# Second batch's scores in float32 from raw q and k in a fused attention, dense and routed layer kernel

## The chip, the cores and the metric

The kernel runs on one core of one Trainium2 chip. The metric is the time of one execution on the device in microseconds, as the median of several runs. Engines are named as in the profile: PE is TensorE (PEld its weight loads), DVE is VectorE, ACT is ScalarE, POOL is GpSimd, and SP is SyncE, which issues most transfers.

## The reference, cut to what matters

```
# q, k, v: float32 (4 batches, 8 heads, 576 positions, 64 wide)
scores = matmul(q, k.T) / 8
kth    = the 32nd largest score of each row
attn   = softmax over the scores >= kth (the others are masked)
x      = attn @ v, heads laid side by side: 2304 rows of 512

x = ((x @ w_a) * (x @ w_b)) @ w_out                 # 512 -> 1536 -> 512
e = argmax(x @ w_gate); g = its softmax weight       # 8 experts
out = g * (relu(x @ w1[e]) @ w2[e])                  # 512 -> 1024 -> 512
```

Which scores pass as the 32 largest, and which expert a row goes to, depend on small differences. So the kernel keeps products near float32 accuracy: it either feeds TensorE float32 operands, or splits an operand into a rounded part and a remainder and adds three cheaper products.

## The kernel before

The work runs in three layers: attention of the four batches, the dense layer of the four batches (`moe1`), and the eight experts (`expert`).

**Attention.** It is cut into units of one pair of heads: batch 0 has eight (its two groups of rows are units of their own, 320 and 256 rows), batches 1 to 3 have four each. A unit's q and k come by DMA as `rawq` and `rawk` (128 partitions, one head on each half, two buffers each). TensorE makes the scores of one half of the columns for both heads at a time, into the only buffer `sp` in PSUM (`score`, L521; L502 for the last 64 rows of both heads, the M tile). This is called a score step below; a pair of heads has eight of the first kind, and one for its M tile. ScalarE copies `sp` to `s` (L527), VectorE forms pairwise maxima and minima `m` and `n` (L535), finds the 32nd largest by MAX8 and MATCH_REPLACE8 (L546 to L573), and masks (L601, which reads the scores `s` and the exponentials `e`, both in SBUF). TensorE transposes the masked rows (L627) and multiplies by v (L648); the result is normalized and written to `xf`.

**How q and k are fed.** `prep_unit` has two ways, chosen by `u.f`, that is by the unit's number in `FU`. With `u.f`, the scores are one float32 product from `rawq` and `rawk`. Without it, ScalarE rounds each to `kH` and `qH` (L464), GpSimd forms the remainders `kL` and `qL` (L465), and a score step has three products, kH·qH, kH·qL and kL·qH. `FU` is `range(8)`: batch 0 alone has the first way. A float32 product stands in the trace as two records, each of the other three as one.

**The dense layer as fill.** When a batch's attention is done, its dense layer gives TensorE 576 matmuls on L748 and 288 on L778, in runs of six; these are called fills below. They are placed between the next batch's attention work. The fills of batch 0 also need the float64 weights, which are converted on the chip during batches 0 and 1 (`conv`, ACT L383/L387, VectorE L385/L388, GpSimd L391/L397) and stored to `ws` and `wos` in DRAM. The fills of batch 3 and the experts follow the attention.

**What sets the order.** No order is written out. Every step is recorded with an engine, a cost and a place `pos`; `Plan.emit` then steps through its own model of the engines, each time giving a free engine the ready step with the lowest `pos`, and the resulting order is what each engine executes. Attention steps have `pos` from 0 up, fills 1e5 more, so that attention goes first where both are ready. `score` is given a cost of 780 with `u.f` and 540 without; the split steps have costs of their own. Changing them shifts the whole order behind. Each engine executes its order strictly, so a step that waits holds up all behind it on its engine.

```
    P(PE, 780 if u.f else 540, pos, score, r=u.q + u.k, w=[sp], label=f"score{u.b}")
```

Of the kernel before, what the change touches and what calls it, by code (L numbers as in the profile page):

```python
# [209 lines left out]
def fused_kernel(ctx: ExitStack, tc: tile.TileContext, q, k, v, w_a, w_b, w_out, w_gate, w1, w2, qx, kx, vx, out,  # L210
                 opts=None, dbg=None):
    nc = tc.nc
    opts = opts or {}
# [15 lines left out]
    HB = FB // 2  # L229
    CW = 512  # L230
    HALVES = opts.get("halves", (0,))
    FU = opts.get("fu", range(8))
    PE, ACT, DVE, POOL, SP = "PE", "ACT", "DVE", "POOL", "SP"

    dram = ctx.enter_context(tc.tile_pool(name="dram", bufs=1, space=bass.MemoryType.DRAM))
# [192 lines left out]
    def load_unit(ui, b, p, groups, pos, after=None):  # L428

        u = Rec()  # L430
        u.b, u.p, u.f, u.first = b, p, ui in FU, ui == 0
        u.raw = {}
# [1105 lines left out]
```

## Time and profile before

| | |
|---|---|
| median of 3 runs | 1207.14 us (1203.96 to 1209.49) |
| profiled execution, its own time | 1207.8 us |
| its span | 1206.1 us |
| PE busy | 1082.9 us, 90% of the span, 7586 instructions |
| DVE busy | 894.5 us, 74% |
| ACT busy | 678.6 us, 56% |
| POOL busy | 462.5 us, 38% |
| chain that ended last | PE 53%, DVE 23%, issue 9%, DMA 6%, ACT 4%, POOL 3% |

Busy shares are means over stages with different limits, so they are read by stretch. In the trace, the scores of batch 0 run until 204 us, those of batch 1 from 211 to 398, and the attention of the other two ends near 788. Up to about 300 us VectorE is busy all the time and TensorE is not; from 344 on TensorE is nearly always busy.

### The profile page before, as it was taken

The page shows a single profiled execution, that of the slowest core. Times are in us where ns is not written, and L with a number is a line of the kernel's source. Part 1 is how long each engine was busy: PE and PEld are TensorE (multiplying, and loading weights), DVE is VectorE, ACT ScalarE, POOL GpSimd, SP SyncE. Part 2 cuts the span into 40 slices and gives each one's busy share as a digit, 9 for nine tenths or more (in the row PEclk, how much of TensorE's full clock was granted, in tenths as well). Part 3 has the DMA queues.
Part 4 walks back from the last instruction along what each step waited for, and adds up shares of the span by engine and source line. Part 5 has one row for each costly group of instructions (what it writes and reads, how often), then busy time and mean ns, then how long its engine had stood idle before and what let it go on. Part 6 is the DMA issues. An engine that isn't in the chain of part 4 may idle for free.

```text
span 1206.1 us, 21828 instructions
## 1 busy us (share of the span) xinstructions
PE 1082.9 (90%) x7586; PEld 942.3 (78%) x7586; DVE 894.5 (74%) x2636; ACT 678.6 (56%) x1442; POOL 462.5 (38%) x620
## 2 busy tenths in 40 slices
PE   3555696887999999999999999998999999999997
PEld 1333474765788789889888888898998999999996
DVE  6999999999989999999999999920005554544441
ACT  6667676775666666666666655723224454554551
POOL 3555577654445444134646313535134100000001
PEclk9766796987999999999999999999999999999999
DMA  7586577996666423333334242245735555554450
GB/s 260 172 311 200 177 250 252 364 311 205 233 235 208 171 96 114 135 115 120 130 104 137 79 144 78 80 167 206 253 126 177 180 151 191 179 163 148 160 177 21
DMA packets 90476, 210.47 MB, mean 175 GB/s; under 512 B 7363, under 2 KB 44611, under 8 KB 82677
## 3 DMA queue, kind: packets, MB, share of 16 engines
q1 hardware_dynamic: 87141, 199.53, 49.2%
q0 software_dynamic: 3216, 9.46, 2.1%
q8 instruction: 62, 1.02, 0.3%
q14 instruction: 57, 0.47, 0.1%
HBM read 174.31 MB, written 35.25 MB: 174 GB/s over the span
## 4 chain that ended last, share of the span: by engine, by line
PE 53%; DVE 23%; issue 9%; DMA 6%; ACT 4%; POOL 3%; SPq 0%; POOLq 0%; DVEq 0%; ACTq 0%
PE ab L748 18%; PE ab L778 10%; DVE m L559 5%; PE ab L1109 4%; DVE kt L562 4%; DVE am L601 4%; PE pv L648 3%; PE sp L521 3%; PE tp L627 3%; PE ms L1158 2%; PE pv L1158 2%; DMA xsort<-rows,pi 2%; DMA out_dram<-y,ti 2%; DVE m L535 1%; DVE n L535 1%
## 5 line engine op out<-in xcount | busy, mean ns | idle before, releaser
L748 PE MATMUL ab<-xh,wt 128*128 128x320 f32 (+1 forms) x1344 | 302.9, 306 | 3.9 <-ACT sb L733 3.9
L748 PEld LDWEIGHTS ab<-xh,wt 128*128 128x128 f32 x1344 | 226.3, 191 | 17.8 <-issue 11.1
L748 PE MATMUL ab<-xl,wt 128*128 128x320 f32 (+1 forms) x672 | 200.0, 298 | 1.4 <-POOL xl L718 1.4
L559 DVE MATCH_REPLACE8 m<-kt,m 128x288 f32<-128x288 f32 x432 | 188.5, 440 | 0.0
L562 DVE MAX8 kt<-m 128x8 f32<-128x288 f32 x432 | 182.1, 444 | 0.4
L778 PE MATMUL ab<-gH,wt 128*128 128x320 f32 (+1 forms) x768 | 169.4, 304 | 2.9 <-DMA wt<-wos 2.9
L756 POOL TENSOR_TENSOR sa<-sa,sb 128x320 f32<-128x320 f32 (+1 forms) x96 | 82.9, 864 | 154.9 <-ACT sb L733 147.8
L601 DVE SCALAR_TENSOR_TENSOR am<-s,kt,e 128x576 f32<-128x576 f32 x144 | 137.9, 983 | 0.0
L778 PEld LDWEIGHTS ab<-gH,wt 128*128 128x128 f32 x768 | 127.8, 190 | 10.7 <-issue 6.4
L748 PEld LDWEIGHTS ab<-xl,wt 128*128 128x128 f32 x672 | 128.9, 192 | 1.6 <-POOL xl L718 1.6
L554 ACT ACTIVATE e<-s,nm 128x576 f32<-128x576 f32 x144 | 108.9, 781 | 16.8 <-POOL nm L549 15.6
L778 PE MATMUL ab<-gT,wt 128*128 128x320 f32 (+1 forms) x384 | 113.8, 296 | 0.0
L1183 POOL DMA_INDIRECT out_dram<-y,ti x23 | 22.9, 997 | 227.6 <-ACT y L1177 208.7
L1027 DVE TENSOR_TENSOR wp<-raw,wp 128x1024 fp32r<-128x1024 f32 (+1 forms) x73 | 67.4, 943 | 52.8 <-ACT wp L1026 52.6
L527 ACT COPY s<-sp 128x576 f32<-128x576 f32 x128 | 81.9, 640 | 40.5 <-PE sp L521 37.5
L627 PE MATMUL tp<-idr,am 128*128 128x128 f32 x512 | 82.3, 299 | 19.4 <-DVE am L601 16.0
L397 POOL TENSOR_TENSOR gT<-sa,gH 128x320 fp32r<-128x320 f32 (+1 forms) x96 | 83.9, 874 | 40.6 <-ACT gH L396 40.4
L631 ACT COPY aT<-tp 128x512 f32<-128x512 f32 x128 | 71.4, 588 | 41.9 <-PE tp L627 41.6
L627 PEld LDWEIGHTS tp<-idr,am 128*128 128x128 f32 x512 | 63.0, 153 | 37.5 <-DVE am L601 18.9
L521 PE MATMUL sp<-rawk,rawq 64*128 64x288 f32 x128 | 37.6, 666 | 60.3 <-DVE n L534 21.9
L1109 PE MATMUL ab<-xgh,wp 128*128 128x304 f32 (+6 forms) x352 | 89.8, 313 | 1.5 <-DVE gT L1116 0.9
L648 PE MATMUL pv<-aT,vt 128*64 128x320 f32 (+1 forms) x512 | 80.4, 458 | 4.2 <-ACT aT L616 3.4
(280 smaller groups left out, 2409.0 us busy)
## 6 DMA issues: line engine op xcount, KB each, us to landing
wt<-ws SPq DMA_DIRECT2D x54, 1024.0 KB, 5.5
wt<-wos SPq DMA_DIRECT2D x44, 768.0 KB, 4.3
raw<-in_moe_w_dram SPq DMA_DIRECT2D x64, 512.0 KB, 3.8
xsort<-rows SPq DMA_DIRECT2D x8, 771.0 KB, 13.1
wp<-ws SPq DMA_DIRECT2D x6, 1024.0 KB
rawk<-in_kx_dram SPq DMA_DIRECT2D x19, 320.0 KB, 5.7
rawq<-in_qx_dram SPq DMA_DIRECT2D x19, 320.0 KB, 3.7
vt<-in_vx_dram SPq DMA_DIRECT2D x20, 288.0 KB, 2.8
```

The lines of the kernel that those rows point to most:

```text
L397: P(POOL, c_pool(cost), pos, lambda: nc.gpsimd.tensor_sub(lo(), src(), fr(hi())), r=rd + wh, w=wl)
L527: P(ACT, c_act(S), pos, lambda hf=hf, sp=sp: nc.scalar.copy(s()[:, :, hf * HS:(hf + 1) * HS], sp()[:, :, 0:HS]), r=[sp], w=[(s, (h, hf)) f ...
L554: P(ACT, c_act(S, True) + 90, pos, lambda h=h, e=e: nc.scalar.activation(e(), s()[:, h], AF.Exp, bias=nm()[:, h], scale=SCALE), r=[(s, (h, ...
L559: P(DVE, c_dve(HS), pos + 5.0 * h, lambda x=x, h=h, j=j: nc.vector.match_replace(out=m()[:, h], in_to_replace=kt(j, 8 * x - 8, 8 * x), in_ ...
L562: P(DVE, c_dve(HS), pos + 5.0 * h, lambda x=x, h=h, j=j: nc.vector.max(out=kt(j, 8 * x, 8 * x + 8), in_=m()[:, h]), r=[(m, h)], w=[KT(j, x)])
L601: P(DVE, c_dve(S) + 60, pos, lambda: nc.vector.scalar_tensor_tensor(am(), sc(), kth(), e(), op0=OP.is_ge, op1=OP.mult, accum_out=r.sum()[: ...
L627: res = nc.tensor.transpose(tp()[:, 512 * h + x * 128:512 * h + (x + 1) * 128], z()[:, 640 * h + x * 128:640 * h + (x + 1) * 128], idf)
L648: nc.tensor.matmul(pv()[64 * h:64 * h + 64, 0:n], u.vt()[:, 256 * h + 64 * j:256 * h + 64 * j + 64], r.aT[h]()[:, j, 0:n], start=(j == 0), ...
L748: res = nc.tensor.matmul(pa()[:, 0:n], view()[:, m, wi, ko, :], xv()[:, ko], start=(ko == 0 and x == 0), stop=(ko == KO - 1 and x == 2))
L756: P(POOL, c_pool(n), pos, lambda: nc.gpsimd.tensor_mul(sa()[:, 0:n], sa()[:, 0:n], sb()[:, 0:n]), r=[sb], w=[sa])
L778: res = nc.tensor.matmul(pa()[:, 0:n], wv()[:, wi, f, :], gv()[:, f, :], start=(f == 0 and x == 0), stop=(f == HB - 1 and x == 2))
L1109: res = nc.tensor.matmul(pa()[:, 0:cap], p1[ko]()[:, wi, f * 128:(f + 1) * 128], xv()[:, ko], start=(ko == 0 and i == 0), stop=(ko == KO - ...
```

## The change

`FU` becomes `range(12)`, so the four units of batch 1 (numbers 8 to 11) are fed the first way. Their eight roundings (L464) and eight remainders (L465) are gone; their 32 score steps on L521 and the 4 of their M tiles on L502 have one float32 product in place of three, and read `rawk` and `rawq`, whose buffers come free after the unit's last score instead of after its split. Batches 2 and 3 keep the split.

```diff
-    FU = opts.get("fu", range(8))
+    FU = opts.get("fu", range(12))
```

The planner makes a new order from there on. Three places follow.

TensorE in batch 1, first unit, between the M tile's score and the next score step (`xh`, `xl` and `wt` are the fill's operands, `am` a masked row that is transposed). Before, where the run of fills ends:

```order
L748 MATMUL ab<-xl_516,wt 128x320
L748 MATMUL ab<-xh_511,wt 128x320
L521 MATMUL sp<-kH,qH 128x288 x2
L521 MATMUL sp<-kH,qL 128x288 x2
L521 MATMUL sp<-kL,qH 128x288 x2
L627 MATMUL tp<-idr,am 128x128 x8
```

After, at the same score step:

```order
L748 MATMUL ab<-xl_516,wt 128x320
L748 MATMUL ab<-xh_511,wt 128x320
L521 MATMUL sp<-rawk,rawq 128x288 x2
L627 MATMUL tp<-idr,am 128x128 x8
L636 MATMUL pv<-idr,am 128x128
L748 MATMUL ab<-xh_511,wt 128x320
```

The three products are one; counted back to the M tile's score, 18 fills stand ahead of this step before, and 42 after.

GpSimd where batch 0 ends and the first units of batch 1 are prepared (L397 and L391 work on converted weights and on the dense layer, L698 on `xf`). Before:

```order
L397 TENSOR_TENSOR gT_1344<-sa,gH_1335 128x320
L465 TENSOR_TENSOR kL<-rawk,kH 128x640
L698 TENSOR_TENSOR xf<-xc,rs 128x256
L391 TENSOR_TENSOR x_1355<-x_1355,xl_1434 128x512
L756 TENSOR_TENSOR sa<-sa,sb 128x320
L465 TENSOR_TENSOR qL<-rawq,qH 128x640
L397 TENSOR_TENSOR gT_1344<-sa,gH_1335 128x320
L397 TENSOR_TENSOR xl_1434<-x_1355,xl_1434 128x512
```

After:

```order
L397 TENSOR_TENSOR gT_1344<-sa,gH_1335 128x320
L698 TENSOR_TENSOR xf<-xc,rs 128x256
L391 TENSOR_TENSOR x_1355<-x_1355,xl_1434 128x512
L756 TENSOR_TENSOR sa<-sa,sb 128x320
L397 TENSOR_TENSOR xl_1434<-x_1355,xl_1434 128x512
L397 TENSOR_TENSOR gT_1344<-sa,gH_1335 128x320
```

The two remainders are gone and the other steps close up.

TensorE at the change from batch 1 to batch 2, behind the last product with v of batch 1 (L652; the M tile is that of batch 2's first unit, with the split in both kernels). Before:

```order
L652 MATMUL pv<-aTt,vt 64x256 x2
L690 MATMUL pv<-idr,rr_101 128x128 x2
L502 MATMUL sp<-kH,qH 128x288 x2
L502 MATMUL sp<-kH,qL 128x288 x2
L502 MATMUL sp<-kL,qH 128x288 x2
L627 MATMUL tp<-idr,am 128x128 x4
L748 MATMUL ab<-xh_4286,wt 128x256
L748 MATMUL ab<-xl_4300,wt 128x256
L748 MATMUL ab<-xh_4286,wt 128x256 x2
L748 MATMUL ab<-xl_4300,wt 128x256
L748 MATMUL ab<-xh_4286,wt 128x256
L627 MATMUL tp<-idr,am 128x128 x4
```

After:

```order
L652 MATMUL pv<-aTt,vt 64x256 x2
L502 MATMUL sp<-kH,qH 128x288 x2
L502 MATMUL sp<-kH,qL 128x288 x2
L502 MATMUL sp<-kL,qH 128x288 x2
L690 MATMUL pv<-idr,rr_101 128x128 x2
L627 MATMUL tp<-idr,am 128x128 x8
L636 MATMUL pv<-idr,am 128x128
L748 MATMUL ab<-xh_4119,wt 128x256
L748 MATMUL ab<-xl_4134,wt 128x256
```

The broadcast for the norm (L690) stands behind the M tile's score now, and the transposes of both masked rows stand ahead of the first fill. Counted up to this M tile's score there are 888 fills in both kernels; up to the score step behind it 942 before and 924 after.

## Rows read from the trace of the kernel before

**Rows 1.** Busy time by stretch; header names columns, then granted clock and DMA.

```profile
core 0: us, PE busy (x) PEld busy (x) DVE busy (x) ACT busy (x) POOL busy (x), PEclk, DMA share, GB/s
184.00:211.00 27.00, 15.70 (x73) 9.35 (x73) 27.00 (x71) 15.00 (x30) 18.70 (x17) 0.62 0.72 246
...
240.00:270.00 30.00, 24.07 (x162) 19.71 (x163) 29.86 (x90) 22.93 (x51) 16.96 (x18) 0.89 0.94 311
270.00:300.00 30.00, 22.86 (x142) 18.07 (x142) 27.51 (x86) 15.88 (x31) 14.42 (x21) 0.77 0.63 205
300.00:344.00 44.00, 41.79 (x337) 35.50 (x335) 43.97 (x153) 27.24 (x63) 22.18 (x37) 1.00 0.62 218
344.00:404.00 60.00, 59.85 (x487) 50.68 (x485) 54.87 (x173) 40.52 (x95) 27.09 (x41) 1.00 0.70 248
404.00:426.00 22.00, 17.91 (x129) 13.50 (x121) 22.00 (x82) 13.30 (x29) 10.43 (x16) 0.92 0.24 81
426.00:785.00 359.00, 356.81 (x2732) 309.68 (x2730) 341.14 (x1097) 226.09 (x510) 151.44 (x217) 1.00 0.32 112
```

**Rows 2.** Waits of VectorE, 184 to 404 us: total, times, longest.

```profile
DVE m L535 <- ACT s L527: 6.8, 3, 3.8
```

**Rows 3.** Groups of instructions: the split, all three batches; busy, mean ns, idle before.

```profile
L465 POOL TENSOR_TENSOR qL<-rawq,qH 128x640 fp32r<-128x640 f32 x12 | 19.6, 1636 | 0.9 <-ACT qH L464 0.9
...
L465 POOL TENSOR_TENSOR kL<-rawk,kH 128x640 fp32r<-128x640 f32 x12 | 18.7, 1562 | 11.2 <-ACT kH L464 7.6 <-DMA wt<-ws 3.6
...
L464 ACT CAST kH<-rawk 128x640 fp32r<-128x640 f32 x12 | 8.7, 728 | 0.1
```

**Rows 4.** Timeline of POOL: start, length, and the instruction.

```profile
188.49 1.72 POOL L465 TENSOR_TENSOR qL<-rawq,qH 128x640 fp32r<-128x640 f32 x1
...
309.76 1.56 POOL L465 TENSOR_TENSOR qL<-rawq,qH 128x640 fp32r<-128x640 f32 x1
```

**Rows 5.** Timeline of DVE: L388 and L601 beside those, and apart from them.

```profile
189.10 1.66 DVE L388 SCALAR_TENSOR_TENSOR gT<-gT 128x512 int32<-128x512 int32 x1
...
213.54 0.67 DVE L388 SCALAR_TENSOR_TENSOR x<-xl,x 128x512 int32<-128x512 int32 x1
...
284.93 0.81 DVE L601 SCALAR_TENSOR_TENSOR am<-s,kt,e 128x576 f32<-128x576 f32 x1
...
310.26 1.67 DVE L601 SCALAR_TENSOR_TENSOR am<-s,kt,e 128x576 f32<-128x576 f32 x1
```

**Rows 6.** Timeline of PE: a float32 score step of batch 0 between fills.

```profile
161.70 0.31 PE L748 MATMUL ab<-xh,wt 128*128 128x320 f32 x1
161.94 0.76 PE L521 MATMUL sp<-rawk,rawq 64*128 64x288 f32 x4
162.62 0.41 PE L748 MATMUL ab<-xh,wt 128*128 128x320 f32 x1
```

**Rows 7.** Timeline of PE: a split score step of batch 1 between fills.

```profile
300.47 0.31 PE L778 MATMUL ab<-gT,wt 128*128 128x320 f32 x1
300.62 0.31 PE L778 MATMUL ab<-gH,wt 128*128 128x320 f32 x1
300.86 0.40 PE L521 MATMUL sp<-kH,qH 64*128 64x288 f32 x2
...
301.45 0.42 PE L778 MATMUL ab<-gH,wt 128*128 128x320 f32 x1
```

**Rows 8.** Timeline of PE: score steps at the lower clock, float32 first, then split.

```profile
202.79 1.33 PE L521 MATMUL sp<-rawk,rawq 64*128 64x288 f32 x4
204.28 0.69 PE L648 MATMUL pv<-aT,vt 128*64 128x256 f32 x2 [0.16 <-ACT aTt L638]
...
244.71 0.61 PE L521 MATMUL sp<-kH,qH 64*128 64x288 f32 x2 [5.00 <-DVE kt L573]
...
245.87 1.97 PE L627 MATMUL tp<-idr,am 128*128 128x128 f32 x8
```

**Rows 9.** Waits of the DMA queue SP, 205 to 420 us: total, times, longest.

```profile
SPq L435 <- POOL kL L465: 8.5, 4, 2.8
```

## The prediction

> **What bounds the kernel now.** I read the busy times by stretch first, because the shares of the whole span mix stages [rows 1]. Between 184 and 211 us VectorE is busy all 27.00 us while TensorE has 15.70, at a granted clock of 0.62; from 240 to 300 VectorE has 57.4 of 60 and TensorE 46.9; from 300 to 344 VectorE 43.97 of 44 and TensorE 41.79. So up to 344 us VectorE sets the pace and TensorE has time to spare. From 344 to 404 it turns: TensorE 59.85 of 60, VectorE 54.87, because the fills of batch 0 have to be done before batch 1's can begin. From 404 to 426 VectorE is full again (22.00) and TensorE is not (17.91): batch 1's dense layer is only just coming in. From 426 to 785 TensorE has 356.81 of 359, and it stays the last one to the end. So the edit has an effect on the time if the start of that last stage, at about 426 us, comes earlier or later, or if more fills are left by then. The same work stands behind it in both kernels.
>
> I then asked what VectorE waits for before 404 us: in all 6.8 us, in three waits for ScalarE's copy of the scores [rows 2]. None is for the split. The split itself is cheap to find: a remainder takes GpSimd 1.56 to 1.64 us, a rounding ScalarE 0.73 [rows 3]. Batch 1 has eight of each, 12.8 us of GpSimd and 5.8 us of ScalarE, and neither engine is near full in any stretch of batch 1 [rows 1]. This time by itself gains nothing. What the split costs VectorE, and what float32 costs TensorE, decide.
>
> **The split's cost to VectorE.** A remainder reads two tensors from SBUF, and so do VectorE's L601 and L388. The rows beside each other show what happens: a remainder runs from 188.49 for 1.72 us, and the L388 that starts at 189.10 takes 1.66 us where one apart from GpSimd's long work takes 0.67; another runs from 309.76 for 1.56, and the L601 at 310.26 takes 1.67 in place of 0.81 [rows 4, 5]. Beside batch 1's eight remainders stand five such stretched rows, of which these are the first (+0.99) and the last (+0.86); the five together are 3.4 us too long. All are before 344 us, where VectorE is the bound, so what is given back counts in full. It is not all given back: the order shows GpSimd's other steps closing up, and these read SBUF too and can meet an L601 in the same way. The bounds are 0 and 3.4; I take **-2.4**, nearer to the upper, because nothing is added to GpSimd in place of the eight.
>
> The Trainium skill has the same rule, in "SBUF — State Buffer", section "Who interferes with whom": a VectorE instruction with two SBUF inputs and a GpSimd instruction that reads SBUF exclude each other, and the later one blocks until the other has ended. The trace agrees: L388 at 189.10 ends about its own 0.67 us after the remainder's end at 190.21 [rows 4, 5].
>
> **The score steps on TensorE.** Start to start, a float32 step between fills takes 162.62 - 161.94 = 0.68 us [rows 6], a split one 301.45 - 300.86 = 0.59 [rows 7]. So a step is 0.09 us longer at the full clock. At the lower clock the two are 204.28 - 0.16 - 202.79 = 1.33 and 245.87 - 244.71 = 1.16, or 0.17 longer [rows 8]. For the 36 steps (four M tiles taken at the same price) that is 3.2 us of TensorE, with bounds of 0 and 6.1. Up to 344 us it goes into TensorE's spare time, 13 us between 240 and 300 alone [rows 1]. On the path are the 13 steps between 344 and 404: 13 x 0.09 = **+1.2**; if TensorE were the bound from 300 on, it would be about 22 steps and +2.0.
>
> The Trainium skill, "FP8 and Floating Point Precision", section "TensorE Precision Notes", speaks against the change: true float32 takes four passes through the array, where the split has three products. By that a step would be 0.59 x 4/3 = 0.79, an estimate from that page, and the 13 steps +2.6 in place of +1.2. The row of 0.68 is measured and decides.
>
> **The order of the fills.** The planner's new order moves fills forward. Counted over TensorE's whole order, 282 fills stand ahead of batch 1's ninth score step before and 342 after; at the fourteenth both have 360, at the 25th (about 344 us) it is 594 and 606, and at batch 2's first step both have all 864. So TensorE does 60 fills in time that it now spends waiting, above all in the 5.00 us ahead of the step at 244.71 [rows 8], and then stands still a little later for want of the converted weights. This gains nothing by itself. What remains is that 12 fewer are left for the stretch from 344 to 404, where TensorE is the bound. A fill takes 300.62 - 300.47 = 0.15 us there [rows 7], so this is 12 x 0.15 = **-1.8**; the bound is 0, if TensorE doesn't get ahead in fact.
>
> **The change to batch 2.** At the M tile of batch 2's first unit both have done 888 fills, at the next step 942 and 924. VectorE is nearly full in this part in the kernel before [rows 1], so attention can't use the place of the 18 fills quickly, and TensorE loses part of 18 x 0.15 = 2.7 us and has the 18 to do later. The bounds are 0 and +2.7; I take **+1.7**, since VectorE is full up to 426 and has 18 of 359 us free after it.
>
> **Transfers.** `rawk` and `rawq` stay taken until the last score, so that the load two units later waits in SP's queue for TensorE and no longer for GpSimd (now 8.5 us in four waits [rows 9]); behind it stand the loads of `wt`, which have three buffers. In 184 to 404 us no fill waits for such a load for long. I put it at 0; if a load came late, it would cost up to its longest wait now, 2.8 us.
>
> **The sum.** -2.4 + 1.2 - 1.8 + 1.7 = -1.3 us, against the profiled execution's own 1207.8 (span 1206.1, and 1.7 around it): 1206.5. That execution lies 0.7 above the median of the runs, 1207.14, so I forecast **1205.8**. With every term at its better or worse end it is -5.2 (-3.4 + 0 - 1.8 + 0) to +7.5 (0 + 2.0 + 0 + 2.7 + 2.8), or 1202 to 1214.6; all terms at one end is unlikely, and 1202 to 1210 is the forecast's own range.
>
> **The rivals.** A measurement of this kernel can tell about 0.5%, 6.0 us, from no change: below 1201.1 is faster, above 1213.2 slower.
>
> *Attention gains more.* The 6.8 us of VectorE's waits before 404 come from where a score step stands among fills and transposes [rows 2]. The order there is new, and with fills moved forward a score may stand free. If the relief is the full 3.4, the two longest waits (some 6 us) go, and the change to batch 2 costs nothing, it is -9.4 - 0.6: near 1197. For it speaks that TensorE gets ahead; against it, that a planner knows of no stretched rows, so its order fits the actual times no better than now. Chance 0.22.
>
> *The longer run of fills stalls VectorE (slower).* Behind the first M tile of batch 1, 42 fills stand ahead of the next score step in place of 18, and TensorE executes strictly in order. The 24 more take 24 x 0.15 = 3.6 us at the full clock, inside the 5.00 us that TensorE waits there [rows 8]. At the lower clock, by the ratio of the steps 1.33 to 0.68, all 42 take 42 x 0.29 = 12.2 us against 18 x 0.15 = 2.7 now, so 9.5 more against 5.0 of slack: VectorE would be stalled for 4.5 us. With the change to batch 2 at +2.7, the steps at +1.2 and no relief, it is +8.4: near 1215.5. It decides by the granted clock at the run: in stretch 240 to 270 the mean is 0.89, in 184 to 211 it is 0.62 [rows 1]. TensorE is busier with the run than without it, so I give it 0.14.
>
> *Float32 dearer than the row.* If a step cost four thirds, the sum is +1.4 more, 1207.2: inside the forecast, 0.05 of its chance. That the change doesn't do what it says is excluded: the order has no L464 or L465 in batch 1.
>
> **How the numbers follow.** The forecast has 0.64, the faster rival 0.22, the slower 0.14, and these are the three chances as well, since each one's time lies in its own class. For 8 in 10 the range reaches into both rivals: 1198.5 to 1212.5.
>
> **What would show it.** In the profile after: float32 steps of 0.68 in batch 1; no stretched L601 beside an L465 before batch 2; the first full stretch of TensorE in batch 2 beginning 1 to 3 us earlier; TensorE idle for 1 to 3 us more just behind batch 2's first M tile; VectorE's waits for ScalarE's copy again some 7 us up to batch 2. I am wrong if these waits come out several us longer or shorter, if TensorE's clock falls in another place, or if it waits after 426 us.

## The result, and the profile after

The changed kernel takes 1215.91 us (median of 8 runs, 1213.17 to 1221.6), the kernel before 1206.72 beside it. The ratio is 1.0084 [1.007, 1.0098]: slower by about 10 us, beyond the 0.5% that a measurement of this kernel can tell. The forecast of 1205.8 and its range up to 1212.5 were wrong. One of the eight executions of the kernel before took 1356.58 us; the ratio leaves it out, and it is not the ratio of the two medians, which lie 9.2 us apart. In a second set of runs the ratio was 1.0083 [1.0063, 1.0104].

The profiled execution of the changed kernel took 1216.07 us, with a span of 1214.4. Its busy time by stretch, with the columns of [rows 1]:

```profile
184.00:211.00 27.00, 16.04 (x92) 11.23 (x89) 27.00 (x71) 14.74 (x29) 16.03 (x15) 0.81 0.82 263
...
240.00:270.00 30.00, 24.50 (x153) 19.27 (x153) 29.57 (x82) 22.67 (x50) 18.82 (x23) 0.94 0.98 324
270.00:300.00 30.00, 25.36 (x147) 19.11 (x146) 29.21 (x94) 14.69 (x30) 10.03 (x15) 0.83 0.63 224
300.00:344.00 44.00, 41.80 (x306) 32.76 (x305) 43.61 (x151) 26.32 (x61) 19.61 (x34) 0.96 0.53 178
344.00:404.00 60.00, 56.80 (x427) 46.33 (x427) 53.92 (x169) 39.29 (x91) 24.86 (x37) 1.00 0.61 223
404.00:426.00 22.00, 17.82 (x123) 13.10 (x120) 20.98 (x76) 13.42 (x28) 11.84 (x16) 0.88 0.42 167
426.00:785.00 359.00, 355.16 (x2707) 306.16 (x2704) 341.59 (x1094) 224.62 (x504) 144.99 (x210) 1.00 0.32 110
```

Up to 344 us the picture is that of [rows 1]: VectorE full, TensorE with time to spare. The first thing to see is 344 to 404. TensorE was busy 59.85 of these 60 us, and now it is 56.80; the 3.2 us are lost on the engine that is the bound there. Its waits from 344 to 430 us, before (total, times, longest; five shorter ones follow, the list sums to 4.0):

```profile
PE tp L627 <- ACT aT L631: 1.0, 1, 1.0
PE ms L952 <- DVE gb L933: 1.0, 1, 1.0
...
```

After (the whole list, 7.3 in sum):

```profile
PE pv L648 <- ACT aTt L638: 2.7, 1, 2.7
PE tp L627 <- ACT aT L631: 2.1, 2, 1.1
PE tp L627 <- DVE am L601: 1.5, 2, 1.1
PE ms L917 <- DVE gb L901: 1.0, 1, 1.0
```

Transposes (L627) and the product with v (L648) now wait for a mask or for ScalarE's copies. The score step of batch 2's first M tile, from which on TensorE stays full, started at 424.14 before:

```profile
424.14 0.53 PE L502 MATMUL sp<-kH,qH 128*128 128x288 f32 x2 [0.46 <-DVE n L535]
```

and starts 4.1 us later after:

```profile
428.28 0.53 PE L502 MATMUL sp<-kH,qH 128*128 128x288 f32 x2
```

The second thing is what is left after the attention. L778's fills, counted in the two stretches 426 to 792 and 792 to 1000 us (time, TensorE's busy time and count for L778 alone), before:

```profile
426.00:792.00 366.00, 78.31 (x522) 1.00 0.33 114
792.00:1000.00 208.00, 47.95 (x342) 0.98 0.51 178
```

and after:

```profile
426.00:792.00 366.00, 71.29 (x480) 1.00 0.32 112
792.00:1000.00 208.00, 55.02 (x384) 0.98 0.52 180
```

At 792 us 42 more fills are still to do. Of all the fills, 1020 stand behind the last score step in the trace of before and 1044 in this one. So 24 of the 42 are put off by the order; the other 18 are late because attention is.

VectorE's waits for ScalarE's copy from 184 to 404 us are as long as in [rows 2], in more pieces:

```profile
DVE m L535 <- ACT s L527: 7.1, 5, 4.5
```

### The profile page after: what moved, and what is told of

Same layout as the page of the kernel before. It is cut to its first block, busy times and chain, and to the rows that moved or that the text cites. A ratio compares the mean times of both kernels' runs of the same rounds, so it can differ in the third digit from the quotient of the medians.

```text
span 1214.4 us, 21663 instructions
## 1 busy us (share of the span) xinstructions
PE 1089.4 (90%) x7514; PEld 941.0 (77%) x7514; DVE 897.1 (74%) x2636; ACT 674.9 (56%) x1434; POOL 450.1 (37%) x612
## 4 chain that ended last, share of the span: by engine, by line
PE 55%; DVE 22%; ACT 6%; issue 6%; POOL 5%; DMA 5%; SPq 0%; POOLq 0%; DVEq 0%; ACTq 0%
PE ab L748 16%; PE ab L778 10%; PE ab L1109 6%; DVE m L559 5%; DVE kt L562 4%; DVE am L601 4%; PE ms L1158 3%; PE pv L648 3%; PE pv L1158 3%; PE tp L627 3%; PE sp L521 3%; DVE n L535 2%; DMA xsort<-rows,pi 2%; DVE m L535 1%; DVE kt L546 1%
## 5 line engine op out<-in xcount | busy, mean ns | idle before, releaser
L748 PE MATMUL ab<-xh,wt 128*128 128x320 f32 (+1 forms) x1344 | 306.2, 308 | 3.9 <-ACT sb L733 3.6
L778 PE MATMUL ab<-gH,wt 128*128 128x320 f32 (+1 forms) x768 | 170.5, 305 | 3.2 <-DMA wt<-wos 3.2
L601 DVE SCALAR_TENSOR_TENSOR am<-s,kt,e 128x576 f32<-128x576 f32 x144 | 142.6, 1017 | 0.1
L778 PEld LDWEIGHTS ab<-gH,wt 128*128 128x128 f32 x768 | 129.4, 192 | 12.8 <-issue 7.8
L521 PE MATMUL sp<-rawk,rawq 64*128 64x288 f32 x256 | 63.5, 570 | 69.9 <-DVE n L534 20.4
L778 PE MATMUL ab<-gT,wt 128*128 128x320 f32 (+1 forms) x384 | 114.6, 299 | 0.0
L397 POOL TENSOR_TENSOR gT<-sa,gH 128x320 fp32r<-128x320 f32 (+1 forms) x96 | 84.5, 880 | 37.9 <-ACT gH L396 37.7
L627 PE MATMUL tp<-idr,am 128*128 128x128 f32 x512 | 80.7, 297 | 16.1 <-DVE am L601 12.2
L521 PEld LDWEIGHTS sp<-rawk,rawq 64*128 64x128 f32 x256 | 25.0, 231 | 89.4 <-issue 40.6
L627 PEld LDWEIGHTS tp<-idr,am 128*128 128x128 f32 x512 | 63.2, 153 | 33.8 <-ACT aT L631 10.5
```

Source lines behind the costliest of these rows:

```text
L397: P(POOL, c_pool(cost), pos, lambda: nc.gpsimd.tensor_sub(lo(), src(), fr(hi())), r=rd + wh, w=wl)
L521: res = nc.tensor.matmul(sp()[:, h, 0:HS], qp()[a, c * 128:(c + 1) * 128], kp()[a, k0 + hf * HS:k0 + (hf + 1) * HS], start=(x == 0), stop= ...
L601: P(DVE, c_dve(S) + 60, pos, lambda: nc.vector.scalar_tensor_tensor(am(), sc(), kth(), e(), op0=OP.is_ge, op1=OP.mult, accum_out=r.sum()[: ...
L627: res = nc.tensor.transpose(tp()[:, 512 * h + x * 128:512 * h + (x + 1) * 128], z()[:, 640 * h + x * 128:640 * h + (x + 1) * 128], idf)
L748: res = nc.tensor.matmul(pa()[:, 0:n], view()[:, m, wi, ko, :], xv()[:, ko], start=(ko == 0 and x == 0), stop=(ko == KO - 1 and x == 2))
L778: res = nc.tensor.matmul(pa()[:, 0:n], wv()[:, wi, f, :], gv()[:, f, :], start=(f == 0 and x == 0), stop=(f == HB - 1 and x == 2))
```

## The experiments

Three things come with the change: other work (no split, a float32 step), a plan without the split's steps, and a plan in which a score step has float32's price. The theory was first that the work costs it, then that the order does, in two places: what is placed between batch 1's attention steps, and how many fills are put off behind batch 2's first M tile. In the kernels that keep a step in the plan and don't execute it, the step is recorded with an empty body, so that the order of all other instructions stays.

**The work alone.** Float32 scores in batch 1, no split, every other instruction in the order of before:

```diff
-            P(ACT, c_act(n, True), p0, lambda raw=raw, hi=hi: nc.scalar.copy(hi(), raw()), r=[raw], w=[hi])
+            P(ACT, c_act(n, True), p0, (lambda: None) if u.fr else lambda ...
-            P(POOL, c_pool(n), p0, lambda raw=raw, hi=hi, lo=lo: nc.gpsimd.tensor_sub(lo(), raw(), fr(hi())),
+            P(POOL, c_pool(n), p0, (lambda: None) if u.fr else lambda ...
-        return [(u.q[0], u.k[0])] if u.f else [...]
+        return [(u.raw["q"], u.raw["k"])] if u.f or u.fr else [...]
```

(`u.fr` holds for units 8 to 11; `rawk` and `rawq` have four buffers.)

> Batch 1's scores are one float32 product from rawq and rawk and its split is gone, as in the change, but every other instruction stands on every engine in the order of the kernel before (the planner is still told of the split and of the old score price; rawq and rawk have four buffers, so that no load waits longer). Theory A, the new order is what costs: the work itself is nearly neutral, the 36 steps' 3.3 us on TensorE are hidden in part and some of the stretched L601 go: 0.995 to 1.002 of the kernel before. Theory B, the work itself costs (dearer scores and GpSimd's other steps meeting L601): 1.005 to 1.009, near the change's 1.0084.

Measured: 1208.75 us, ratio 1.0019 [1.0007, 1.0031]. The work costs 2.3 us of the 10; the other 8 come from the order.

The same with the split still executed, its results unused (only the last of the three edits):

> Float32 scores in batch 1 in the order of the kernel before, with its split still computed by ScalarE and GpSimd and not used: the price of the float32 steps alone. Theory A: at most 13 steps of 0.09 us and the M tiles are on the path, 1.000 to 1.002. Theory B: the steps' whole 3.3 us and the waits behind them, 1.003 to 1.006.

Measured: 1209.8 us, ratio 1.0016 [1.0, 1.0032]. So with float32 steps, taking the split away gains nothing that can be seen.

The other corner: the order and the step lengths of before, without the eight remainders (each product of a score step of batch 1 also has its own `start` and `stop`, so that only the last one stays):

```diff
+            P(POOL, c_pool(n), p0, (lambda: None) if u.fr else lambda ...
-        return [(u.q[0], u.k[0])] if u.f else [...]
+        return [(u.q[0], u.k[0])] * (3 if u.fr else 1) if u.f or u.fr else [...]
```

> The order and the score steps' length of the kernel before, without batch 1's eight remainders on GpSimd: each of its score steps multiplies the rounded kH and qH three times and keeps the last product, so the remainders' part of batch 1's scores is left out. What taking GpSimd's eight passes away gives by itself. My prediction's term: 2.4 us less, 0.997 to 0.999. Rival: other GpSimd steps meet L601 in their place and nothing is gained or something lost, 1.000 to 1.003.

Measured: 1205.86 us, ratio 0.9989 [0.998, 0.9998], or 1.3 us gained. So the relief of VectorE is 0 to 1.3 us, and the price of the float32 steps 1.9 us (split executed in both) to 3.6 us (from this kernel to the work alone). Masking with L601 shows a relief of the same size. Busy time of L601 over the same 84 rows from 204 us on (length of the stretch, busy time, count), in the kernel before, with the split executed unused, and with the work alone:

```profile
204.00:429.00 225.00, 40.71 (x84) 0.94 0.70 244
```

```profile
204.00:431.00 227.00, 39.87 (x84) 0.95 0.70 242
```

```profile
204.00:429.00 225.00, 38.90 (x84) 0.96 0.70 244
```

This kernel, without the remainders, has 39.33 us. So in the old order L601 is 0.5 to 1.8 us shorter without batch 1's eight remainders, less than the 2.4 us of the prediction.

**The price in the plan.** The changed kernel, with batch 1's score steps at the split's price (its M tiles at 900 in place of 980 in the same way):

```diff
-                P(PE, 780 if u.f else 540, pos, score, r=u.q + u.k, w=[sp],
+                P(PE, (540 if u.b else 780) if u.f else 540, pos, score, r=u.q + u.k, w=[sp],
```

> The change, with the planner told that a float32 score step of batch 1 costs what a split one does (540 and 900 in place of 780 and 980). The order behind batch 1 has again as many fills ahead of each score step as the kernel before (984 ahead of batch 2's ninth, where the change has 966). Theory A, the 18 to 24 fills that the change leaves for later are what costs: 1.000 to 1.004. Theory B, the work: 1.007 to 1.010, as the change.

Measured: 1214.44 us, ratio 1.0059 [1.0043, 1.0074], between the two expected ranges. In this order no fills are put off: 1020 stand behind the last score step, as before. So the price is worth 1.0084 - 1.0059, 0.25% or 3.0 us, and 1.0059 - 1.0019, 0.40% or 4.8 us, come from a plan that has no split in it; by the intervals each is good to about 0.2%.

**Half the change.** Only units 8 and 9, the first two of batch 1:

```diff
-    FU = opts.get("fu", range(8))
+    FU = opts.get("fu", range(10))
```

> FU is range(10): only the first two units of batch 1 are fed in float32, units 10 and 11 keep the split. The planner's order then has the early half of the change (60 more fills at the fourteenth... of batch 1's score steps seen from the ninth on: 6 more at step 41, 60 at step 45, 24 from step 51 on) but no fills put off behind batch 2's first M tile. Half the work of the change costs about half of the 0.19% that the whole work costs in the old order, 1.1 us. Theory 'two places' (fills drawn forward before 300 us slow attention of batch 1 by some 3 us, and fills put off behind batch 2's first M tile cost 3.5 us): 1.1 + 3 = about +4 us, ratio 1.003 to 1.004. Theory 'only the fills put off': +1 us, ratio 1.001. Theory 'only batch 1's order': +6 to +7 us, ratio 1.005 to 1.006.

Measured: 1206.08 us, ratio 0.9992 [0.9979, 1.0004]. Up to batch 1's third unit this order is that of the changed kernel, with up to 60 fills drawn forward. It costs nothing, and the theory of two places, which had put 3 us on these fills, is wrong in that part.

Only units 10 and 11 (`FU` is `(*range(8), 10, 11)`):

> FU is 0 to 7, 10 and 11: only the last two units of batch 1 are fed in float32. The order up to batch 1's 20th score step is that of before; from there fewer fills are drawn forward (6 to 24 fewer), and 18 to 24 are put off behind batch 2's first M tile, as in the whole change. Theory 'two places': half the work 1.1 us and 24 fills x 0.147 = 3.5 us: about +4.6 us, ratio 1.003 to 1.004, with the score step 108 not more than 2 us later than before. Theory 'only the fills put off': +6 us, ratio 1.005, most of it after the attention. Theory 'only batch 1's order': +1 us, ratio 1.001.

Measured: 1210.1 us, ratio 1.0022 [1.0009, 1.0036], or 2.7 us. This kernel puts off 24 fills (1044 behind the last score step), and these cost about as much by the next experiments; the last two units alone lose nothing further. Yet TensorE waits here from 344 to 404 us as it does in the changed kernel:

```profile
PE tp L627 <- ACT aT L631: 1.5, 1, 1.5
PE tp L627 <- DVE am L601: 0.7, 1, 0.7
...
```

So a list of such waits does not yet say what a kernel loses by them.

**Fills put off, the work untouched.** The kernel before, with the planner told 520 for a split step in place of 540 (and 880 for 900 for an M tile):

```diff
-                P(PE, 780 if u.f else 540, pos, score, r=u.q + u.k, w=[sp],
+                P(PE, 780 if u.f else 520, pos, score, r=u.q + u.k, w=[sp],
```

> The kernel before with its own work, split and all; only the planner's prices of a split score step are 520 and 880 in place of 540 and 900. Its order is that of before up to batch 2's first M tile; behind it 30 to 42 fewer fills are drawn between the score steps, and 36 of them are left over after the attention. Theory 'the fills put off cost their time': 36 x 0.147 = +5.3 us, ratio 1.004, with the score steps of batches 2 and 3 at the times of before and the end later by 5 us. Theory 'fills put off cost nothing, because attention is earlier by as much': ratio 1.000, score steps 5 us earlier and the same end.

Measured: 1213.61 us, ratio 1.0044 [1.0029, 1.0059]: 5.3 us for 36 fills (1056 behind the last score step). The expectation had the order of before up to batch 2's first M tile; in the trace TensorE's order differs from that of before at some places from 235 us on.

With 535 and 895, 24 fills are put off, as many as in the changed kernel:

> The kernel before with its own work, split and all; the planner's prices of a split score step are 535 and 895 in place of 540 and 900. Its fills stand as in before up to batch 2's first M tile; behind it 18 fewer are drawn, and 24 are left over after the attention, as many as in the changed kernel. Theory 'a fill put off costs its time': 24 x 0.147 = +3.5 us, ratio 1.003. Theory 'the 36 fills of the run with prices of 520 and 880 cost what they did because of something else in that order': ratio 1.000 to 1.001.

Measured: 1209.79 us, ratio 1.0021 [1.001, 1.0031], 2.5 us. Here TensorE's order is that of before up to the M tile of batch 1's last unit, at 380 us. Per fill the two give 0.15 and 0.10 us; the fill of [rows 7] takes 0.15. So fills that are put off cost two thirds of their time or all of it, and the attention is not much earlier in return: from batch 2's first M tile to the M tile of batch 3's last unit it takes 327.9 us before, 328.9 with 36 fills put off and 326.8 with 24. The planner's step is a jump: 5 of 540 in a price moves 24 fills.

Both orders also have no fill between L636 and the product L648 ahead of batch 2's first M tile, as the changed kernel has none, and TensorE waits there; with 535:

```profile
PE pv L648 <- ACT aTt L638: 1.3, 1, 1.3
```

So what happens at this M tile can come with a price alone, and it is part of the 5.3 and 2.5 us.

Float32's price in the plan, the plan's split kept, none executed (with the edits of the first experiment, and the M tiles' price in the same way):

```diff
+                P(PE, 780 if u.f or u.fr else 540, pos, score, r=u.q + u.k, w=[sp],
```

> The scores of batch 1 in float32, no split executed; the planner still reckons with the split's steps on ScalarE and GpSimd (which are empty) and gives batch 1's score steps the prices of float32, 780 and 980. So this has the order that the price alone makes: no fills drawn forward before step 48, 6 to 30 fewer from there to batch 2, and 24 to 36 put off behind batch 2's first M tile. Work alone, in the old order: 1.0019. Theory 'two places': 1.0019 and 30 x 0.147 = 4.4 us, ratio 1.0055, all of the added time after the attention. Theory 'only the split's absence from the plan': 1.002. If the price alone made the whole loss, 1.008.

Measured: 1213.09 us, ratio 1.0043 [1.0028, 1.0058]. Beside the work alone this is 0.24%, 2.9 us, for 36 fills (1056 behind the last score step), or 0.08 us each: less than the 4.4 us expected, and as much as the price was worth above.

**The order of units 10 and 11.** The whole work of the change, but in the plan units 10 and 11 keep the split's steps (empty) and its price; units 8 and 9 are planned as in the change:

```diff
-    FU = opts.get("fu", range(8))
+    FU, FR = opts.get("fu", range(10)), range(10, 12)
```

(with the edits of the first experiment, `u.fr` now for units 10 and 11.)

> The whole work of the change (all four units of batch 1 in float32, no split executed), but for units 10 and 11 the planner still reckons with the split's steps (empty) and with a score step's price of 540; units 8 and 9 are as in the change. The order is that of the kernel with only units 8 and 9 changed, which took 0.9992 of the time before: fills drawn forward in the first half of batch 1, none put off behind batch 2's first M tile. Theory 'what is left of the loss is the order of units 10 and 11': only the work of two more units is added, 0.1% or 1.2 us: ratio 1.000 to 1.001, score step 76 at most 1 us later than before. Theory 'what is left is the float32 work of units 10 and 11 itself, where TensorE is the bound': ratio 1.004, score step 76 later by 3 to 4 us.

Measured: 1207.9 us, ratio 1.0011 [0.9998, 1.0025]. The same instructions as in the changed kernel, in another order of the last two units and of what follows, and 0.7% or 8.8 us are gone. (`rawk` and `rawq` have four buffers here and two in the changed kernel. What that gives was not tried by itself; in the changed kernel none of TensorE's waits from 184 to 430 us is for a transfer.) From 344 to 404 us the list of TensorE's waits has one row, where that of the changed kernel has 3.2 us of L627, and that of before has none:

```profile
PE ms L875 <- ACT rows L869: 1.1, 1, 1.1
```

TensorE's timeline shows what the order does in two places. Unit 10's transposes in the changed kernel:

```profile
361.53 0.61 PE L627 MATMUL tp<-idr,am 128*128 128x128 f32 x4
363.26 0.66 PE L627 MATMUL tp<-idr,am 128*128 128x128 f32 x4 [1.12 <-DVE am L601]
```

and in this kernel:

```profile
359.83 0.61 PE L627 MATMUL tp<-idr,am 128*128 128x128 f32 x4
360.19 0.36 PE L748 MATMUL ab<-xh,wt 128*128 128x256 f32 x1
...
360.86 0.28 PE L748 MATMUL ab<-xh,wt 128*128 128x256 f32 x1
361.17 0.66 PE L627 MATMUL tp<-idr,am 128*128 128x128 f32 x4
```

Between the two groups of transposes stand six fills here and none there, so the mask (`am`) of the second has more time to come. The mask is also slower there: 2.08 us beside a remainder of batch 2 on GpSimd, and 1.27 here.

The other two of the changed kernel's three waits at L627 cannot be read from TensorE's order in this way. Ahead of one stand six fills, ahead of the other a score step, and both end with ScalarE's copy:

```profile
373.09 0.28 PE L748 MATMUL ab<-xh,wt 128*128 128x256 f32 x1
374.36 0.65 PE L627 MATMUL tp<-idr,am 128*128 128x128 f32 x4 [0.99 <-ACT aT L631]
...
392.12 0.76 PE L521 MATMUL sp<-rawk,rawq 64*128 64x288 f32 x4
393.95 0.66 PE L627 MATMUL tp<-idr,am 128*128 128x128 f32 x4 [1.08 <-ACT aT L631]
```

In this kernel the neighbours of the second stand in the same order, and nothing waits:

```profile
390.07 0.76 PE L521 MATMUL sp<-rawk,rawq 64*128 64x288 f32 x4
390.75 0.66 PE L627 MATMUL tp<-idr,am 128*128 128x128 f32 x4
```

Why the copy holds up the one and not the other stays open. Just ahead of batch 2's M tile, the changed kernel:

```profile
421.30 0.27 PE L636 MATMUL pv<-idr,am 128*128 128x128 f32 x1
424.27 3.50 PE L648 MATMUL pv<-aT,vt 128*64 128x256 f32 x16 [2.71 <-ACT aTt L638]
```

and ScalarE in the same time:

```profile
421.39 0.46 ACT L396 CAST gH<-sa 128x320 fp32r<-128x320 f32 x1 [0.65 <-POOL sa L756]
422.02 0.78 ACT L554 ACTIVATE e<-s,nm 128x576 f32<-128x576 f32 x1 [0.17 <-POOL nm L549]
...
423.95 0.28 ACT L638 COPY aTt<-pv 128x128 f32<-128x128 f32 x1
```

The transposes were done at 421.57; their last copy (L638) comes at 423.95, behind five other steps of ScalarE (the first two stand here), and the product stands right behind them on TensorE. In the kernel with the old plan for units 10 and 11 a score step and six fills lie between:

```profile
416.44 0.42 PE L636 MATMUL pv<-idr,am 128*128 128x128 f32 x1
416.79 0.61 PE L521 MATMUL sp<-kH,qH 64*128 64x288 f32 x2
...
417.81 0.55 PE L748 MATMUL ab<-xh,wt 128*128 128x320 f32 x1
...
419.02 1.95 PE L648 MATMUL pv<-aT,vt 128*64 128x256 f32 x16
```

But TensorE waits in this part in every one of these kernels, if not here then elsewhere: from 404 to 430 us it is busy 21.89 of 26 us before, 21.82 in the changed kernel and 21.61 in this one. So the 2.71 us cannot be booked as lost beside the kernel before.

**The changed kernel once more,** to see which of these rows are the kernel's and which one execution's:

> The changed kernel once more, for a second profile of it and a second ratio. Ratio 1.007 to 1.010 again. If what the first profile showed is the kernel's and not that execution's, then score step 54 starts within 1 us of before, step 66 some 3 us and step 76 some 4 us later, TensorE idles for about 3 us between steps 60 and 72, and the time after step 143 is 3.5 to 4.5 us longer than before. If step 76 is less than 2 us late at the same ratio, the loss is not in batch 1's attention.

Measured: 1215.63 us, ratio 1.0083 [1.0063, 1.0104]. The longest waits of TensorE from 344 to 430 us:

```profile
PE pv L648 <- ACT aTt L638: 2.5, 1, 2.5
PE tp L627 <- DVE am L601: 2.1, 2, 1.2
PE tp L627 <- ACT aT L631: 2.1, 2, 1.1
```

They are back in place and size. Other things were not: batch 1's 19th score step started 4.1 us later than before here and 0.2 later in the first profile, and batch 2's M tile is late by 5.7 us in place of 4.1:

```profile
429.85 0.49 PE L502 MATMUL sp<-kH,qH 128*128 128x288 f32 x2 [1.20 <-DVE kt L573]
```

With prices of 535 and 520, where all work up to there is that of before, this M tile starts at 424.88 and 426.63. So a single start in one profile can be off by 2 to 4 us, and ratios over many runs must carry the shares.

## Why the prediction was wrong

In all, the runs put the 10.1 us down as: work 2.3, plan without the split 4.8, float32's price in the plan 3.0. The forecast had -1.3 in their place. By its own steps:

**What bounds the kernel** was read right. At the M tile of batch 1's third unit, near 335 us, the changed kernel is 1.2 and 3.1 us late in its two profiles, but has 18 more fills done; what follows from there on decides.

**The split's cost to VectorE** (-2.4) was too large: 0 to 1.3 us. The pairs of [rows 4, 5] are real, but what they showed is where two passes met in one execution. In the new order L601 meets GpSimd's steps no less often. Over the same 84 rows its sum in the changed kernel is 43.90 us against 40.71, although eight remainders are gone. 15 of its passes take over 1 us, before 14, and 12 and 11 of these stand beside another step of GpSimd than a remainder:

```profile
204.00:430.00 226.00, 43.90 (x84) 0.94 0.69 237
```

This is not what makes the kernel slower: with the old plan for units 10 and 11 the sum is 43.78, at 1.0011 of the time before. The lower bound of the range, 0, was the better value, for the reason that the text itself gave (GpSimd's other steps close up) and then set aside. The rule of the Trainium skill ("SBUF — State Buffer", "Who interferes with whom") holds row by row; it says which two instructions exclude each other, and not that fewer of one kind leave fewer meetings.

**The float32 step** had its price right and its cover wrong. In batch 1 of the changed kernel it takes 351.38 - 350.70 = 0.68 us, as forecast, and not the 0.79 that was estimated by the four passes of the Trainium skill ("FP8 and Floating Point Precision", "TensorE Precision Notes"):

```profile
350.70 0.76 PE L521 MATMUL sp<-rawk,rawq 64*128 64x288 f32 x4
351.38 0.39 PE L778 MATMUL ab<-gH,wt 128*128 128x256 f32 x1
```

But 1.9 to 3.6 us came through, where the forecast let 1.2 through and the 36 steps in all are worth 3.2. Spare time of TensorE before 344 us hid at most a part of the step. VectorE is the bound there, and it can only go on when a score step has ended; that is an explanation and was not tried by itself. Relief and price together were -1.2 in the forecast and are +2.3: 3.5 us of the miss.

**The order of the fills** is the step that failed (-1.8 forecast, +4.8 measured, 6.6 us of the miss). The term counted how many fills stand ahead of each score step, and took a fill drawn forward as a fill less to do. The fills drawn forward in the first two units gained and cost nothing, as the text said. What failed is the gain: 12 fills fewer behind 344 us were to give time on the engine that is the bound there, and TensorE instead lost 3.2 us from 344 to 404 to waits at L627, where before it had none and with the old plan for units 10 and 11 1.1 us. The count of fills ahead of L521 can't show such waits. The order of after against before, read at each L627 and L648, was at hand and would have shown some of them: one of the three at L627 and the one ahead of batch 2's M tile, where nothing stands between. The other two at L627 have fills or a score step between.

**The change to batch 2** was the right mechanism with a size too small: +1.7 forecast, 3.0 us by the price taken back, 2.5 to 5.3 us for 24 to 36 fills put off on purpose. The upper bound stood at 2.7 for 18 fills; 24 are left in the end. Attention did not use the place of the missing fills: a fill that is put off is done later. The wait of 2.7 us ahead of the M tile, which the prediction did not have, belongs to this part, since a price alone brings a wait at this place too (1.3 us).

**Transfers** at 0: in the lists of TensorE's waits from 184 to 430 us none is for a transfer. SP's queue waited for a score step in place of the remainder, 6.4 us in three waits.

**The slower rival** came out at about its time, 1215.5, and not by its mechanism. It had the clock fall at the run of 42 fills and VectorE stall. But TensorE still waits behind that run:

```profile
245.13 0.76 PE L521 MATMUL sp<-rawk,rawq 64*128 64x288 f32 x4 [2.08 <-DVE kt L573]
```

The run fitted into the 5.00 us of [rows 8] and left 2.08; VectorE was busy 29.57 of 30 us, at a granted clock of 0.94. Two of the rival's terms, no relief and the change to batch 2 at its upper end, were true. The faster rival fell: the waits for ScalarE's copy are as long as they were.

**What stays open.** Neither half of the change shows the 4.8 us, once the fills put off are taken out; they need the first two units' new order and the last two's together. In the changed kernel the waits at L627 can stand for about 2 us of them (3.2 us, against 1.1 with the old plan for units 10 and 11), though the kernel with units 10 and 11 alone has such waits too and loses nothing by them that can be seen. In the kernel with the split's price they lie elsewhere: there batch 0's fills are used up when batch 1 has two score steps left, and TensorE waits 1.72 us for VectorE:

```profile
398.71 0.85 PE L521 MATMUL sp<-rawk,rawq 64*128 64x288 f32 x2 [1.72 <-DVE n L535]
```

So two orders lose about the same with different waits. How much of the 4.8 us each single wait is worth was not tried, and where the rest of them lies is not known.

## What to carry to other kernels

Where a planner makes the order, cost an edit in two parts: the work in the old order, and the old work in a new order; here the first was 2 us and the second 8. Read a new order at the places where the bounding engine needs something from another engine (here each transpose and product), and ask what lies between the two; counting the cover work ahead of one kind of step doesn't show it. Read the other engine's order too: two of three waits here do not show in TensorE's alone. A step that vanishes from the plan can be left in it with an empty body: with that done for two of the four units, the whole change took 1.0011 of the time before, in place of 1.0084. And compare sums of a trace over the same rows, since a fixed window can cut some off in the slower kernel.

## What the runs showed of the hardware

Two things were not expected. Taking GpSimd's eight passes away shortened VectorE's masked passes by little in the same order, from 40.71 and 39.87 us over 84 rows to 39.33 and 38.90; in the order of the changed kernel they took 43.90. And after the 2.71 us in which TensorE stood still ahead of batch 2's M tile, its 16 products took 3.50 us in one execution, at a granted clock of 0.53 over that stretch, and 1.95 us in the other, at 1.00, after 2.48 us of standing still:

```profile
424.20:427.70 3.50, 3.42 (x16) 1.72 (x16) 3.50 (x11) 1.23 (x3) 1.08 (x1) 0.53 0.19 75
```

```profile
426.10:429.50 3.40, 2.53 (x20) 1.25 (x20) 3.40 (x9) 1.55 (x3) 1.08 (x1) 1.00 0.20 77
```

A granted clock of 0.53 is nearly the lower of the two levels, 1.2 of 2.4 GHz. After a wait of about the same length the products thus took 1.6 us more in one execution than in the other.
